# Three small edits to an adaLN transformer block: an earlier second normalisation, one maximum moved inside three steps, five casts moved from VectorE to ScalarE

## The chip, the cores and the metric

The kernel runs on one core of one Trainium2 chip. A core has a matrix engine (TensorE, PE in the profile), VectorE (DVE), ScalarE (ACT), GpSimd (POOL) and SyncE (SP), which here issues most of the DMA transfers. PSUM holds matmul results, SBUF everything else; a PSUM bank holds 512 float32 numbers on each of 128 partitions. The metric is the device time of one execution in microseconds, lower is better.

## The reference, cut to what matters

```python
mod = (silu(c) @ w_mod).reshape(1, 6, 1, -1)
sa, ca, ga, sb, cb, gb = (mod[:, i] for i in range(6))
h = layernorm(x) * (1 + ca) + sa                 # x: 1 x 2048 x 448
q, k, v = split(h @ wqkv)                        # 16 heads of 28 columns
o = softmax(q @ k.T * 28 ** -0.5) @ v
x = x + ga * (o @ wo)
h = layernorm(x) * (1 + cb) + sb                 # first norm of the second half
y = layernorm(h)                                 # second norm
x = x + gb * (gelu(y @ w1 + b1) @ w2 + b2)       # w1: 448 x 1792, w2: 1792 x 448
```

Float32 accuracy is reached by splitting each factor of most products into a high part rounded to the matrix format (`hi`) and the remainder (`lo`), and adding three products: hi·hi, hi·lo and lo·hi.

## The kernel before, in words

**Three stretches.** Up to about 170 us the kernel computes the first norm, the projections to q, k and v and the first part of the row maxima. From there to about 814 us runs the attention loop, and from there to the end the feed-forward part ("the tail").

**The attention loop.** Its outer loop runs over 16 *units*: unit u is (group g of four heads, query block qt of 512 queries), u = 4g + qt. Inside a unit 16 *steps* (kt) run over key blocks of 128 keys; step number = 16u + kt. A step computes the scores of four heads in two halves of two heads each (line 1305), two exponentials of 128 x 2 x 512 on ScalarE (line 1318), and then the four products of the step before with v (function `av`, line 1263). A head has 28 columns, so a score matmul uses only one of four groups of 32 rows of the matrix engine, and matmuls in different row groups can run at the same time. Half 0 lies in row groups 0 and 1, half 1 in row groups 2 and 3. Each half takes three terms (hi·hi, lo·hi, hi·lo), so a step has 12 score matmuls, two at a time in one half.

**Row maxima.** The softmax needs the maximum of each row before its unit begins. For later units these are computed inside the steps as extra matmuls (line 476) into a small ring of PSUM tiles, each followed by a maximum on VectorE (line 481, or line 686 for two heads at once). `emit_single(half, ...)` takes one waiting maximum, preferably one whose row groups are those of the given half. From step 121 on the kernel is in *ring* mode: a third score tile, s2, takes the two PSUM banks of the ring tile m2, and a step has one single maximum and one pair. The flag `three` is set when no maximum is left, near step 236.

**Projection steps.** When a unit of the last group ends, and also unit 11, its result is divided by the softmax sums and multiplied with `wo`. `unit_end_tasks` spreads this over steps of the next unit: `t_den` (kt 1) and `t_rec` (kt 2) send the sums through memory and take reciprocals, `t_split` (kt 6) multiplies on GpSimd (line 1019), `t_split2` (kt 7) makes hi (a cast, line 1029) and lo (a subtraction on GpSimd, line 1030), and four calls of `t_wo` (kt 8 to 11) multiply with `wo`, one token block of 128 each. A unit is `staged` when its result is only stored for later; units 11 to 15 are not staged. In the steps kt 8 to 11 of units 12, 13 and 14 (`is_wo`), ring mode is off: s2 gives its banks back to m2, and a step has `WO_MAX` = 3 single maxima. `n0` of them are emitted beside the scores of the first half, one behind each of its terms and preferring half 1; the other `n_max - n0` stand behind the last scores of the second half and prefer half 0. For unit 15's results the same tasks run inside the tail.

**Second half.** `ln2_stages(b)` gives, for one of four token blocks b of 512 tokens, the work of the two norms as 14 numbered stages: statistics (0 to 3), first norm with scale and shift (`mid`, 4 to 7), statistics again (6 to 9), second norm (`fin`), and the addition of the output bias (`addb`, 10 to 13, GpSimd). `chunk(k)` then transposes four 128 x 128 tiles on TensorE, copies the result as hi on ScalarE (line 1118) and takes lo on VectorE (lines 1120 and 1122). For b = 0 stage i runs at step 231 + i and the chunks at steps 244 to 247. For b = 1, 2, 3 the stages run beside the 14 feed-forward steps of the block before (stage i in step i), and the chunks at step 13. A feed-forward step is `mlp1` (11 matmuls, line 396, a gelu on ScalarE, hi and lo) and `mlp2` of two steps earlier (12 matmuls, lines 1389 to 1391). `w_prep` splits the weights w1 and w2 on VectorE and ScalarE in the last attention unit and during block 0 of the tail.

**Order.** The order on every engine is the order in which the program issues; each engine works through its own instructions in that order and waits on semaphores. `sched` maps a step to small functions that run at the step's end, in the order in which they were registered.

Of the kernel before, what the change touches and what calls it, by code (L numbers as in the profile page):

```python
# [44 lines left out]
def tile_adaln_block(ctx: ExitStack, tc: tile.TileContext, x, wqkv, wo, w1, b1, w2, b2, c, w_mod, out):  # L45
    nc = tc.nc
    pe, act, dve, pool, sp = nc.tensor, nc.scalar, nc.vector, nc.gpsimd, nc.sync
# [27 lines left out]
    def nm(t):  # L75
        uid[0] += 1
        return f"{t}_{uid[0]}"

    def sbt(tag, shape, dt=F32, bufs=1):
        return sb.tile(shape, dt, tag=tag, name=nm(tag), bufs=bufs)  # L80
# [27 lines left out]
    def ps_mx():  # L108
        mx_ring.append(mx_ring.pop(0))
        return ps_tile(mx_ring[-1], 1 if mx_ring[-1] == "m1" else 2)  # L110

    def ps_o():
        return ps_tile("o")
# [4 lines left out]
    def f(t):  # L118
        return t.bitcast(F32)
# [78 lines left out]
    def ln_stat(mv, t, src):  # L198
        st = sbt("st", [128, 6], bufs=2)
        dve.bn_stats(out=st, in_=src)  # L200
        dve.bn_aggr(out=mv[:, t, :], in_=st)

    def ln_rstd(mv, n):
        ve = sbt("ve", [128, 4], bufs=2)
        dve.tensor_scalar(out=ve[:, :n], in0=mv[:, :n, 1], scalar1=EPS, scalar2=None, op0=ALU.add)
        rs = sbt("rs", [128, 4], bufs=2)
        pool.tensor_tensor(out=rs[:, :n], in0=ve[:, :n], in1=neg_half[:, :n], op=ALU.pow)
        return [(mv[:, t, 0:1], rs[:, t : t + 1], rs) for t in range(n)]
# [7 lines left out]
    def normalise(dst, src, mr):  # L216
        dve.tensor_scalar(out=dst[:, :D], in0=src, scalar1=mr[0], scalar2=mr[1], op0=ALU.subtract, op1=ALU.mult)

    def xn_t():
        return sbt("xn", [128, 512], bufs=4)  # L220
# [54 lines left out]
    def transposes(p, xs, k):  # L275
        for t in range(4):
            pe.transpose(p[:, t * 128 : (t + 1) * 128], xs[t][:, k * 128 : (k + 1) * 128], ident)  # L277
# [114 lines left out]
    def mm_acc(p, terms, mid=None):  # L392
        for i, (a, b) in enumerate(terms):
            if mid and i == len(terms) // 2:
                mid()
            pe.matmul(p, a, b, start=(i == 0), stop=(i == len(terms) - 1))  # L396
# [588 lines left out]
    def last_g(qt):  # L985
        return NG - 2 if qt == NB - 1 else NG - 1
# [8 lines left out]
    def unit_end_tasks(u, o_sb):  # L995
        g, qt = divmod(u, NB)
        st = {}
        staged = g < last_g(qt)
        parts = [g] if g > last_g(qt) else list(range(g + 1))

        def t_den():
            q_ = pool if u == NU - 1 else sp
            den = sbt("den", [128, 16], bufs=2)
            q_.dma_start(den, o_sb[DH:128:32, :].rearrange("j (q r) -> j q r", r=16))
            st["den"] = den

        def t_rec():
            q_ = pool if u == NU - 1 else sp
            rec = st["den"]
            dve.reciprocal(rec, rec)  # L1010
            drec = dr.tile([4, 512], F32, tag="drec", name=nm("drec"), bufs=2)
            q_.dma_start(drec.rearrange("j (q r) -> (j q) r", r=16), rec)
            rb = sbt("osb", [128, 512], bufs=2)
            q_.dma_start(rb, drec[:, None, :].broadcast_to([4, 32, 512]))
            st["rb"] = rb

        def t_split():
            st["on"] = st["rb"]
            pool.tensor_tensor(out=st["on"], in0=o_sb, in1=st["rb"], op=ALU.mult)  # L1019

        def t_split2():
            on = st["on"]
            if u < NU - 1:
                hi = sbt("hi", [128, 512], F32R, bufs=3)
                lo = sbt("lo", [128, 512], F32R, bufs=3)
            else:
                hi = sb.tile([128, 512], F32R, tag=YTAGS[7], name="o_hi", bufs=1)
                lo = sbt("osb", [128, 512], F32R, bufs=2)
            dve.tensor_copy(hi, on)
            pool.tensor_tensor(out=lo, in0=on, in1=f(hi), op=ALU.subtract)  # L1030
            st["hi"], st["lo"] = hi, lo
            if staged:
                for part in range(2):
                    sp.dma_start(f(doh[part][g])[:, qt * 512 : (qt + 1) * 512], f((hi, lo)[part]))

        def t_wo(t):
            def go():
                if t == 3 and mx_ring[0] == "m1" and len(mx_ring) > 1:
                    mx_ring.append(mx_ring.pop(0))
                p = ps_mx()  # L1040
                ts = slice(t * 128, (t + 1) * 128)
                terms = []
                for g_ in parts:
                    if g_ == g:
                        hi, lo = st["hi"][:, ts], st["lo"][:, ts]
                    else:
                        hi, lo = o_in[(qt, g_)][:, 0, ts], o_in[(qt, g_)][:, 1, ts]
                    w_hi, w_lo = wo_p[0][:, g_, :], wo_p[1][:, g_, :]
                    terms += [(hi, w_hi), (hi, w_lo), (lo, w_hi)]
                mm_acc(p[:, :D], terms)  # L1050
                y = sbt("full", [128, 512], bufs=3)[:, :D]
                act.copy(y[:, :D], p[:, :D])
                pool.tensor_tensor(out=acc[qt][:, t, :], in0=acc[qt][:, t, :], in1=y[:, :D], op=ALU.add)

            return go


        times = (0, 3, 9, 10) if staged else (0, 1, 5, 6)
        tasks = list(zip(times, (t_den, t_rec, t_split, t_split2)))
        if not staged:  # L1060
            tasks += [(7 + t, t_wo(t)) for t in range(4)]
        return tasks
# [4 lines left out]
    def ln2_stages(b):  # L1067
        h2 = []
        ys = []

        mv = {}
        mr = {}

        def stat(which, t):
            if t == 0:
                mv[which] = sbt("mv", [128, 4, 2], bufs=2)
            ln_stat(mv[which], t, acc[b][:, t, :] if which == 0 else h2[t])
            if t == 3:
                mr[which] = ln_rstd(mv[which], 4)

        def mid(t):
            yt = xn_t()
            ys.append(yt)
            y = yt[:, :D]
            normalise(y, acc[b][:, t, :], mr[0][t])
            pool.tensor_tensor(out=y, in0=y, in1=rows["cb"], op=ALU.mult)
            pool.tensor_tensor(out=y, in0=y, in1=rows["sb"], op=ALU.add)
            h2.append(y)

        def fin(t):  # L1090
            normalise(ys[t], h2[t], mr[1][t])
            dve.tensor_copy(ys[t][:, D:512], ys[t][:, 384:D])

        def addb(t):
            pool.tensor_tensor(out=acc[b][:, t, :], in0=acc[b][:, t, :], in1=rows["b2g"], op=ALU.add)

        plan = {}
        for t in range(4):
            plan.setdefault(t, []).append(lambda t=t: stat(0, t))
            plan.setdefault(4 + t, []).append(lambda t=t: mid(t))  # L1100
            plan.setdefault(6 + t, []).append(lambda t=t: stat(1, t))
            plan.setdefault(11 + t // 2, []).append(lambda t=t: fin(t))
            plan.setdefault(10 + t, []).append(lambda t=t: addb(t))

        def stage(i):
            for fn in plan.get(i, ()):
                fn()

        def chunk(k):
            if b not in yT:  # L1110
                tiles = [
                    sb.tile([128, 512], F32R, tag=YTAGS[(7 * b + n) % len(YTAGS)], name=nm("y"), bufs=1) for n in range(7)
                ]
                yT[b] = (lambda k: tiles[k] if k < 3 else tiles[6], lambda k: tiles[3 + k])
            p = ps_o() if b and k == 3 else ps_mx()
            transposes(p, ys, k)
            hi = yT[b][0](k)
            act.copy(hi, p)
            if k < 3:
                dve.tensor_tensor(out=yT[b][1](k), in0=p, in1=f(hi), op=ALU.subtract)  # L1120
            else:
                dve.tensor_tensor(out=hi[64:128], in0=p[64:128], in1=f(hi)[64:128], op=ALU.subtract)

        return stage, chunk
# [79 lines left out]
    at(28, b2_mul)  # L1204
    last0 = NKT * (NU - 1)
    lnst = [ln2_stages(b) for b in range(NB)]
    for i in range(14):
        at(last0 - 9 + i, lambda i=i: lnst[0][0](i))
# [30 lines left out]
    def is_wo(s_):  # L1239
        return s_ // NKT >= NU - NB and 8 <= s_ % NKT < 12  # L1240
# [30 lines left out]
    for u in range(NU):  # L1271
        g, qt = divmod(u, NB)
        for kt in range(NKT):
            step = u * NKT + kt
# [15 lines left out]
            more = ring and not three and extra(step)  # L1290
            late_one, after = after, more
            n_max = 0 if ring else WO_MAX if is_wo(step) else 4 - step % 2
            n0 = 1 if step % 4 == 3 and not is_wo(step) else 2
            closing = bool(px_open) and step % 2 == 1

            ks, qs = kst[(g, kt // 4)], qst[u]
# [159 lines left out]
```

## Time and profile before

| what | value |
|---|---|
| median of three runs | 1110.67 us (1110.44 to 1110.94) |
| the profiled execution's own time | 1110.93 us |
| its span, first to last instruction | 1109.0 us |
| granted TensorE clock | 1.000 |
| busy share PE / DVE / ACT / POOL | 99% / 72% / 63% / 19% |
| attention loop | about 172 to 814 us |
| tail | about 814 us to the end |

In the profile, a row of the timeline gives the start in us from the span's start, the duration, engine and line, operation, the tile written and the tiles read, shapes, the number of merged instructions, and in brackets the idle time before it and what ended that. A row of the waits gives the total idle time, the number of times and the longest. The busy share of PE is not a measure of full use, because matmuls are pipelined and their ends modelled; distances between starts are what can be read.

### The profile page before, as it was taken

The numbers are of one execution on the slowest core, as the hardware profiler recorded it, in microseconds if no ns is written. First come the engines' busy times: TensorE is split into PE (matmuls) and PEld (weight loads), VectorE is DVE, ScalarE is ACT, GpSimd is POOL, SyncE is SP. The second block draws the span as 40 slices with busy tenths as digits, with TensorE's granted clock in tenths as the row PEclk, the third lists the DMA queues.
The fourth block names the chain that finished last, engine by engine and source line by source line (L and its number), as shares of the span: only waits on it lengthen the run. The fifth ranks groups of instructions, "written<-read, shape, count | busy, mean of one in ns | idle before, by whom it ended". The sixth has DMA issues, their size and how long they took to land.

```text
span 1109.0 us, 20702 instructions
## 1 busy us (share of the span) xinstructions
PE 1098.7 (99%) x8319; PEld 667.0 (60%) x8319; DVE 800.4 (72%) x1380; ACT 701.6 (63%) x892; POOL 213.0 (19%) x214
## 2 busy tenths in 40 slices
PE   8999999999999999999999999999999999999998
PEld 6756775444444444444444454545568888888887
DVE  6968788999999999988888867584557744434322
ACT  4565657888888888888888878577763411111210
POOL 1533333110000000000000020216215414023000
PEclk9999999999999999999999999999999999999999
DMA  9563264121231211221211402112222100000000
GB/s 309 205 199 97 89 202 113 53 68 30 79 92 44 79 34 54 67 89 49 79 40 59 126 29 87 58 30 78 73 82 67 32 34 1 4 31 1 34 1 34
DMA packets 49341, 81.19 MB, mean 73 GB/s; under 512 B 12311, under 2 KB 18702, under 8 KB 49234
## 3 DMA queue, kind: packets, MB, share of 16 engines
q1 hardware_dynamic: 48762, 79.14, 22.7%
q8 instruction: 65, 1.06, 0.4%
q10 hardware_dynamic: 148, 0.46, 0.1%
q0 software_dynamic: 336, 0.28, 0.1%
q14 instruction: 30, 0.25, 0.1%
HBM read 55.04 MB, written 26.48 MB: 74 GB/s over the span
## 4 chain that ended last, share of the span: by engine, by line
PE 96%; DVE 2%; ACT 1%; DMA 1%; issue 1%; SPq 0%; POOL 0%; ACTq 0%; DVEq 0%; POOLq 0%
PE s L1305 23%; PE o L1263 23%; PE m L396 17%; PE pa L396 9%; PE m L476 8%; PE s L1390 3%; PE s L1391 3%; PE s L1389 3%; PE s L476 2%; PE t L1390 1%; PE t L1391 1%; PE t L1389 1%; PE o L277 1%; DMA slot_c<-in_w_mod_dram 1%; DVE mxp L481 1%
## 5 line engine op out<-in xcount | busy, mean ns | idle before, releaser
L481 DVE TENSOR_REDUCE mxp<-m 128x1 f32<-128x512 f32 x563 | 365.0, 686 | 75.3 <-PE m L476 65.2
L1305 PE MATMUL s<-slot_b,slot_a 28*128 28x512 f32 (+1 forms) x3072 | 358.1, 424 | 0.3 <-ACT slot_c0h L1318 0.3
L1305 PEld LDWEIGHTS s<-slot_b,slot_a 28*128 28x128 f32 (+1 forms) x3072 | 211.4, 184 | 172.1 <-ACT slot_c L1318 93.8
L476 PE MATMUL m<-kh,qh 28*128 28x512 f32 x615 | 229.7, 468 | 0.6 <-DVE mxp L481 0.3
L1318 ACT ACTIVATE slot_c<-s 128x1024 f32<-128x1024 f32 x170 | 174.7, 1027 | 53.4 <-PE s L1305 52.5
L1263 PE MATMUL o<-slot_c,v 128*32 128x512 f32 x680 | 178.9, 605 | 0.0
L1351 ACT ACTIVATE full<-m,b_col 128x512 f32<-128x512 f32 x56 | 38.5, 688 | 193.4 <-PE m L396 180.9
L1263 PE MATMUL o<-slot_c0h,v 128*32 128x512 f32 x512 | 134.7, 605 | 0.0
L1263 PE MATMUL o<-slot_c1h,v 128*32 128x512 f32 x512 | 134.7, 605 | 0.0
L1318 ACT ACTIVATE slot_c0h<-s 128x1024 f32<-128x1024 f32 x128 | 131.6, 1028 | 2.4 <-PE m L396 2.4
L1318 ACT ACTIVATE slot_c1h<-s 128x1024 f32<-128x1024 f32 x128 | 130.8, 1022 | 0.0
L686 DVE TENSOR_REDUCE mxp<-s 128x2 f32<-128x1024 f32 x103 | 126.3, 1226 | 5.1 <-PE s L1305 0.2
L1354 DVE CAST hi<-full 128x512 fp32r<-128x512 f32 x42 | 18.6, 444 | 122.8 <-ACT full L1351 122.8
L1318 ACT ACTIVATE slot_d<-s 128x1024 f32<-128x1024 f32 x86 | 88.4, 1027 | 26.3 <-PE s L1305 25.6
L476 PEld LDWEIGHTS m<-kh,qh 28*128 28x128 f32 x615 | 92.2, 182 | 16.8 <-DVE mxp L481 13.3
L1263 PE MATMUL o<-slot_d,v 128*32 128x512 f32 x344 | 90.5, 605 | 0.4 <-ACT osb L1227 0.4
L1019 POOL TENSOR_TENSOR osb<-osb,osb 128x512 f32<-128x512 f32 x16 | 20.5, 1284 | 365.2 <-DMA osb<-drec 334.8
L396 PE MATMUL m<-y,slot_a 128*128 128x512 f32 x160 | 60.7, 396 | 0.0
L1355 DVE TENSOR_TENSOR lo<-full,hi 128x512 fp32r<-128x512 f32 x56 | 42.4, 758 | 20.5 <-ACT hi L1354 16.5
L481 DVE TENSOR_REDUCE mxp<-ma 128x1 f32<-128x512 f32 x61 | 39.5, 682 | 13.2 <-PE ma L476 7.5
L650 DVE CUSTOM_DVE_ANT_0 slot_d0i<-m,slot_d0i 128x512 f32<-128x512 f32 x54 | 37.3, 691 | 15.1 <-PE m L476 9.2
L1263 PEld LDWEIGHTS o<-slot_c,v 128*32 128x32 f32 x680 | 24.6, 108 | 39.1 <-issue 36.5
(343 smaller groups left out, 1854.4 us busy)
## 6 DMA issues: line engine op xcount, KB each, us to landing
slot_b<-d SPq DMA_DIRECT2D x32, 256.0 KB
slot_a<-d SPq DMA_DIRECT2D x32, 256.0 KB
d<-lo SPq DMA_DIRECT2D x28, 256.0 KB
d<-hi SPq DMA_DIRECT2D x16, 256.0 KB
osb<-drec SPq DMA_DIRECT2D x15, 256.0 KB
out_dram<-xn SPq DMA_DIRECT2D x16, 224.0 KB
raw<-in_B_w_dram SPq DMA_DIRECT2D x14, 224.0 KB
qh<-d SPq DMA_DIRECT2D x12, 256.0 KB
```

Of the source, the lines that this page charges most:

```text
L396: pe.matmul(p, a, b, start=(i == 0), stop=(i == len(terms) - 1))
L476: pe.matmul(m, qh_sb[(g, qt)][js, i * 128 : (i + 1) * 128], k[js, :], start=True, stop=True)
L481: dve.tensor_reduce(out=mxp[(g, qt)][:, i, j, cch : cch + 1], in_=m, op=ALU.max, axis=AX.X)
L686: dve.tensor_reduce(out=mxp[(g, qt)][:, i, j : j + 2, cch], in_=t, op=ALU.max, axis=AX.X)
L1263: pe.matmul(o[32 * j : 32 * j + 32, :], v_sb[kt // 4][:, kt % 4, 4 * g + j, :], p[j // 2][:, j % 2, :], start=(kt == 0), stop=(kt == NKT - 1),
L1305: pe.matmul(s2[:, jj, :], ks[rows_, kp, kc], qs[rows_, qp, :], start=(term == 0), stop=(term == 2))
L1318: act.activation(pt[hf], s2, AF.Exp, scale=SCALE)
L1351: act.activation(gf, p, AF.Gelu_apprx_tanh, bias=b1_col[:, i : i + 1])
L1355: dve.tensor_tensor(out=glo, in0=gf, in1=f(ghi), op=ALU.subtract)
L1389: pe.matmul(pp, ghi[:, ts], w_hi, start=(m == 0), stop=False)
L1390: pe.matmul(pp, ghi[:, ts], w_lo, start=False, stop=False)
L1391: pe.matmul(pp, glo[:, ts], w_hi, start=False, stop=(m == NFT - 1))
```

## The change

Three edits, independent of each other in the code:

1. `t_split2`: for units that are not staged (11 to 15) the cast of the 128 x 512 result to `hi` is issued by ScalarE (`act.copy`) and no longer by VectorE.
2. `ln2_stages`: `fin(t)` runs at stage 10 + t // 2 and no longer at 11 + t // 2, for all four blocks.
3. The attention loop: in the first projection step of a unit (kt 8 in an `is_wo` step) `n0` is 1 and no longer 2. It acts where ring mode is off, in steps 200, 216 and 232: one maximum stands beside the first half's scores and two behind the second half's.

```diff
-            dve.tensor_copy(hi, on)
+            (dve.tensor_copy if staged else act.copy)(hi, on)
             pool.tensor_tensor(out=lo, in0=on, in1=f(hi), op=ALU.subtract)
...
-            plan.setdefault(11 + t // 2, []).append(lambda t=t: fin(t))
+            plan.setdefault(10 + t // 2, []).append(lambda t=t: fin(t))
             plan.setdefault(10 + t, []).append(lambda t=t: addb(t))
...
-            n0 = 1 if step % 4 == 3 and not is_wo(step) else 2
+            n0 = 1 if (kt == 8 if is_wo(step) else step % 4 == 3) else 2
```

## The prediction

> **What bounds the kernel now.** I read the page first, for the engine that ends the span, then TensorE's waits, then the timeline around each edited place.
>
> ```profile
> span 1109.0 us, 20702 instructions
> ...
> PE 96%; DVE 2%; ACT 1%; DMA 1%; issue 1%; SPq 0%; POOL 0%; ACTq 0%; DVEq 0%; POOLq 0%
> ```
>
> The chain that ended last runs 96% through TensorE (PE). So an edit counts only where it moves a start on PE; time taken from or given to VectorE (DVE) or ScalarE (ACT) is free until PE waits for it. PE's waits name two places that the edits touch:
>
> ```profile
> PE m L277 <- DVE xn L217: 0.9, 2, 0.6
> ...
> PE m L396 <- POOL lo L1030: 0.3, 1, 0.3
> ```
>
> The first is a transpose waiting for a second norm, the second a projection waiting for lo. They give idle time only; what a wait costs is read from starts. The third place shows in the starts alone. Step 216, a first projection step (kt 8), on PE, ACT and DVE:
>
> ```profile
> 694.70 0.49 PE L1305 MATMUL s<-slot_b,slot_a 29*128 29x512 f32 x2
> ...
> 695.03 0.39 PE L1305 MATMUL s<-slot_b,slot_a 28*128 28x512 f32 x2
> 695.40 0.49 PE L476 MATMUL m<-kh,qh 28*128 28x512 f32 x1
> ...
> 696.52 0.62 PE L1263 MATMUL o<-slot_c1h,v 128*32 128x512 f32 x2
> ...
> 694.33 1.02 ACT L1318 ACTIVATE slot_c1h<-s 128x1024 f32<-128x1024 f32 x1
> 695.97 1.02 ACT L1318 ACTIVATE slot_d<-s 128x1024 f32<-128x1024 f32 x1 [0.62 <-PE s L1305]
> ...
> 693.81 1.23 DVE L686 TENSOR_REDUCE mxp<-s 128x2 f32<-128x1024 f32 x1
> ```
>
> The second maximum starts at 695.40, 0.05 after step 215's second exponential ended (694.33 + 1.02 = 695.35). That exponential reads s2, whose banks the ring tile m2 has just taken over. First score to first product with v: 696.52 - 694.70 = 1.82. The next step has the same 15 matmuls and no such wait:
>
> ```profile
> 700.16 0.49 PE L1305 MATMUL s<-slot_b,slot_a 29*128 29x512 f32 x2
> 700.17 0.51 PE L476 MATMUL m<-kh,qh 28*128 28x512 f32 x2
> 700.50 0.65 PE L1305 MATMUL s<-slot_b,slot_a 28*128 28x512 f32 x8
> ...
> 700.98 0.41 PE L1305 MATMUL s<-slot_b,slot_a 28*128 28x512 f32 x2
> 701.32 0.62 PE L1263 MATMUL o<-slot_d,v 128*32 128x512 f32 x2
> ```
>
> It takes 701.32 - 700.16 = 1.16: four rounds of up to four matmuls, the last three 0.24 apart ((700.98 - 700.50) / 2), 0.34 from the last round to the product. Steps 200 and 232 are as slow as 216:
>
> ```profile
> 650.29 0.50 PE L1305 MATMUL s<-slot_b,slot_a 29*128 29x512 f32 x2
> ...
> 652.12 0.62 PE L1263 MATMUL o<-slot_c1h,v 128*32 128x512 f32 x2
> ...
> 741.46 0.49 PE L1305 MATMUL s<-slot_b,slot_a 29*128 29x512 f32 x2
> ...
> 743.38 0.62 PE L1263 MATMUL o<-slot_c1h,v 128*32 128x512 f32 x2
> ```
>
> They take 1.83 and 1.92.
>
> **The maximum (n0 = 1).** Only steps 200, 216 and 232 change; nothing is added or removed. The second maximum now stands behind all scores, so the wait for the exponential no longer stops the scores. Next in line is the second half's score tile s0: the pair maximum of step 215 reads it until 693.81 + 1.23 = 695.04. With the 0.05 seen above, the second half starts at 695.09, its two further terms at 695.33 and 695.57, and the product at 695.91, 1.21 from the step's start. By then m2 is free (695.35), so the two late maxima go in the last round, in row groups 0 and 1. Savings: 1.82 - 1.21 = 0.61; with the same shape 0.62 and 0.71 in steps 200 and 232; together 1.94. Both ends: if the s0 wait held the rest up as the old one did, only the earlier release is left, 695.35 - 695.04 = 0.31 a step, 0.93 in all; if nothing waits, all three fall to 1.16, 2.09 in all; if the two late maxima shared a row group, 0.24 a step would go again. I take 1.94, since all waits in it have rows. Their reductions on DVE come later, but the ring tile is needed only in the next step, behind the projection.
>
> One thing speaks against this. If matmuls began strictly in program order, the second half could not begin ahead of the first half's third term, the step would take a fifth round, 1.16 + 0.24 = 1.40, and the three steps would save 1.37. Step 217 bears on it: its second maximum, issued behind the second term's pair, starts at 700.17, ahead of that pair at 700.50. I stay with that row. The Trainium skill, "TensorE: Matmul & The Clock Gate", section The mechanism, states the strict order, in starts and in ends; by it the sum would be 0.57 smaller, and the starts of this trace do not agree with it.
>
> **The cast on ScalarE.** Five casts of 0.42 leave DVE, five of about 0.6 come to ACT (a row of such a cast, 0.59, is below). Behind each on ACT stand the next step's exponentials; it waits for GpSimd's product. Where it pays is step 248:
>
> ```profile
> 787.88 0.59 ACT L1118 CAST y<-m 128x512 fp32r<-128x512 f32 x1
> 788.55 1.02 ACT L1318 ACTIVATE slot_c<-s 128x1024 f32<-128x1024 f32 x1
> ...
> 784.47 1.28 POOL L1019 TENSOR_TENSOR osb<-osb,osb 128x512 f32<-128x512 f32 x1 [7.21 <-DMA osb<-drec]
> 790.87 1.34 POOL L1030 TENSOR_TENSOR lo<-osb,hi 128x512 fp32r<-128x512 f32 x1 [5.12 <-DVE hi L1029]
> ...
> 790.30 0.42 DVE L1029 CAST hi<-osb 128x512 fp32r<-128x512 f32 x1
> ...
> 791.40 0.56 PE L396 MATMUL m<-slot_e,hi 128*128 128x448 f32 x2
> 792.26 0.47 PE L396 MATMUL m<-slot_e,lo 128*128 128x448 f32 x1 [0.30 <-POOL lo L1030]
> 792.66 0.76 PE L1305 MATMUL s<-slot_b,slot_a 29*128 29x512 f32 x8
> ...
> 796.51 0.57 PE L396 MATMUL m<-slot_e,hi 128*128 128x448 f32 x2
> ...
> 797.22 0.74 PE L1305 MATMUL s<-slot_b,slot_a 29*128 29x512 f32 x8
> ```
>
> GpSimd's product is ready at 785.75, but DVE reaches the cast only at 790.30, behind the splitting of w1; lo follows at 790.87 to 792.21, and PE waits. From the products with hi to the next scores it takes 1.26 (792.66 - 791.40), against 0.71 in step 249 (797.22 - 796.51): 0.55 lost. ACT is free for the cast at 787.88 + 0.59 = 788.47 and done near 789.07; lo is ready near 790.5, before its matmul's turn 0.4 after 791.40. The price is on ACT: the exponential of 788.55 moves to about 789.1. Its result is read one step later, behind the projection and the scores of 792.66, so nothing waits. I take 0.55 saved; the ends are 0.55 and 0.
>
> In steps 199, 215 and 231 the cast falls into ACT's idle 0.62 ahead of 695.97 (same shape, three times): 695.35 + 0.6 = 695.95, where the exponential starts today, though by the first edit it could start earlier; again its reader stands behind a projection. That idle time and the projection are the cover; were they gone, each cast would cost PE 0.6, 3.0 for five. In the tail (unit 15) the cast stands four feed-forward steps ahead of its projection, on an ACT that waits for PE's next result: 0.
>
> **The norm one stage sooner.** Nothing is added; four normalisations and four small copies a block move up on DVE, past one feed-forward step's work. They issue no DMA. PE rows at the boundary of blocks 0 and 1, then of 1 and 2, then DVE:
>
> ```profile
> 880.75 0.38 PE L277 MATMUL m<-ident,xn 128*128 128x128 f32 x2
> ...
> 882.93 0.45 PE L1389 MATMUL s<-slot_d0i,hi 128*128 128x448 f32 x1
> ...
> 886.25 0.48 PE L396 MATMUL m<-y,slot_b 128*128 128x512 f32 x1
> ...
> 953.98 1.03 PE L277 MATMUL m<-ident,xn 128*128 128x128 f32 x8
> 954.77 0.45 PE L1389 MATMUL s<-slot_d0i,hi 128*128 128x448 f32 x1
> ...
> 880.37 1.33 DVE L217 TENSOR_SCALAR xn<-xn,mv,rs 128x448 f32<-128x448 f32 x1
> ...
> 885.01 1.29 DVE L1120 TENSOR_TENSOR y<-m,y 128x512 fp32r<-128x512 f32 x2
> ```
>
> Eight transposes take 2.18 (882.93 - 880.75) at the first boundary and 0.79 (954.77 - 953.98) at the second: 1.39 lost, because DVE normalises the third tile only at 880.37. One stage sooner all four are done a feed-forward step (some 5 us) before. What is late next: the first matmuls of block 1 (886.25) would come 1.39 sooner, at 884.86, but their PSUM tile is that of the first transposes, which DVE reads from 885.01 for half of 1.29, until about 885.65. The chain up to there hangs on block 0's last gelu, which doesn't move. So they start near 885.7 and 0.55 is saved; the ends are 1.39 and 0. In blocks 2 and 3 PE doesn't wait here: 0. For block 0 the stages fall in steps 241 and 242, where two more normalisations now stand ahead of unit 14's reciprocal on DVE, and behind it on SP its DMAs, then weight loads:
>
> ```profile
> 777.23 0.24 DVE L1010 RECIPROCAL den<-den 128x16 f32<-128x16 f32 x1
> ...
> 778.49 0.20 DVE L1092 COPY xn<-xn 128x64 f32<-128x64 f32 x1
> ...
> 871.09 0.69 DVE L1355 TENSOR_TENSOR lo<-full,hi 128x512 fp32r<-128x512 f32 x1 [4.40 <-ACT hi L1354]
> ```
>
> What follows the reciprocal until 778.69 goes ahead of it: it comes 778.69 - 777.47 = 1.2 later, and so does GpSimd's product, 786.95 for 785.75: still 1.5 before ACT's turn at 788.47. Cost 0. In stage 10 of block 1 the first normalisations wait for GpSimd's reciprocal square root; DVE is idle there for 4.40, ahead of 871.09, which takes them even at 1.33 each. In blocks 2 and 3 the cover is the same, a feed-forward step between two stages; were it gone, lo would come up to 2.7 late, against two steps until mlp2 reads it.
>
> **Sum.** 1.94 + 0.55 + 0.55 = 3.04. The profiled execution took 1110.93, 0.26 above the median and 1.93 above its span; all three savings lie inside the span, so 1107.89 for that execution and 1107.6 against the median 1110.67. A change of 0.2%, 2.2 us, is about what a measurement of this kernel can tell from none.
>
> **Rivals.**
>
> *The second half waits anyway (no change).* s0 blocks as m2 did: 0.93 for 1.94, in all 2.03, 1108.6. For it: a blocked matmul held up everything behind it at 695.40. Against: s0's release comes 0.31 sooner, and only the second half stands behind it. The same side is reached if either of the 0.55 fails and the maxima give less than 1.7: 1108.5 to 1109.7.
>
> *Strict program order on PE (faster, less).* 1.37 + 0.55 + 0.55 = 2.47, 1108.2, with the rows of step 217 against it. It is what the Trainium skill's section named above would make of this kernel.
>
> *The maxima fall out of step (slower).* The two late maxima are taken for the other half, so the order of all later maxima shifts, in steps 200 to 235. Where two matmuls that ran side by side then need the same row group, the step takes a fifth round, 0.24. Above 13 such steps of 36 the gain of 3.04 is gone; at 22 the kernel is over 0.2% slower; in all 36 it is 1110.67 - 3.04 + 8.64 = 1116.3. For it: the order is made by a planner that nothing in the profile shows for the new order. Against: it asks for a half's own maxima first, and the four projection steps now take seven of one half and five of the other, where they took eight and four.
>
> *ACT is held up (slower).* If GpSimd's product in step 247 came more than 1.5 later than I put it, ACT would stand, and past 2.8 PE too, 1 for 1; past six the gain is gone. For it: GpSimd already idles 7.21 for the transfer ahead of 784.47. Against: only 1.2 of delay has a row.
>
> **How the numbers follow.** My sum 0.62, strict order 0.13: faster 0.75. The second half waits, or a 0.55 fails: 0.13, same. Maxima out of step 0.10, ACT held up 0.02: slower 0.12. The time is my sum's, 1107.6. The low end takes the best ends, 2.09 + 0.55 + 1.39 = 4.03: 1106.6. The high end goes into the cases of no change, 1109.6, and leaves out those of slower and a part of the others.
>
> **What would show it.** Steps 200, 216, 232: first score to first product near 1.2, one L476 in the first round, and no matmul waiting for an exponential; near 1.4 is strict order, near 1.5 the s0 wait. Step 248: the wait for lo gone from PE's list, ACT's cast between 788 and 789 less what was saved before. First block boundary: eight transposes in 0.8, the wait for xn gone, and a new one of some 0.8 for L1120 ahead of block 1's first matmul. Steps 201 to 235 otherwise as long as before. I am wrong if those steps grow, if ACT idles ahead of a cast, or if DVE's earlier normalisations, which wait for GpSimd's reciprocal square root, make mlp2 wait for lo.

## The result and the profile after

The changed kernel takes 1108.99 us (median of 18 runs, 1108.13 to 1109.51) against 1110.81 us for the kernel before on the same chip (18 runs, 1109.99 to 1111.58). The ratio is 0.9983 with a 95% interval of 0.9976 to 0.9990: 1.8 us less, a gain, since the interval leaves out 1, but smaller than the 2.2 us that the prediction took for what can just be told from no change. The profiled execution took 1109.11 us, its span is 1107.1 us, and the granted clock is 1.000 as before.

The chain that ended last:

```profile
PE 97%; DVE 1%; DMA 1%; ACT 1%; issue 0%; SPq 0%; ACTq 0%; DVEq 0%
```

TensorE still sets the time. Its list of waits (total, times, longest):

```profile
PE m L396 <- DVE y L1120: 0.5, 1, 0.5
...
PE s L476 <- DVE mxp L481: 0.4, 1, 0.4
```

The waits for xn (L217) and for lo (L1030) are gone from the list, and these two are new. The first was forecast as what is late next at the block boundary; the second was not forecast at all. The three edited places, one after the other. Step 216 on PE, then ACT and DVE:

```profile
694.15 0.50 PE L1305 MATMUL s<-slot_b,slot_a 29*128 29x512 f32 x2
694.16 0.50 PE L476 MATMUL m<-kh,qh 28*128 28x512 f32 x1
694.49 0.79 PE L1305 MATMUL s<-slot_b,slot_a 28*128 28x512 f32 x8
694.99 0.49 PE L476 MATMUL m<-kh,qh 28*128 28x512 f32 x2
695.11 0.40 PE L1305 MATMUL s<-slot_b,slot_a 28*128 28x512 f32 x2
695.44 0.62 PE L1263 MATMUL o<-slot_c1h,v 128*32 128x512 f32 x2
...
693.92 1.02 ACT L1318 ACTIVATE slot_c1h<-s 128x1024 f32<-128x1024 f32 x1
...
693.26 1.23 DVE L686 TENSOR_REDUCE mxp<-s 128x2 f32<-128x1024 f32 x1
```

One maximum stands in the first round, the other two in one of the last, and no score waits for the exponential of 693.92 any more. From the first score to the first product it takes 695.44 - 694.15 = 1.29, where it took 1.82. Steps 200 and 232 do the same:

```profile
650.52 0.49 PE L1305 MATMUL s<-slot_b,slot_a 29*128 29x512 f32 x2
...
651.81 0.62 PE L1263 MATMUL o<-slot_c1h,v 128*32 128x512 f32 x2
...
740.90 0.50 PE L1305 MATMUL s<-slot_b,slot_a 29*128 29x512 f32 x2
...
742.18 0.62 PE L1263 MATMUL o<-slot_c1h,v 128*32 128x512 f32 x2
```

They take 1.29 and 1.28, for 1.83 and 1.92. With starts in thousandths the three savings are 0.54, 0.54 and 0.65, together 1.73.

Step 248, PE, then ACT and POOL:

```profile
790.61 0.57 PE L396 MATMUL m<-slot_e,hi 128*128 128x448 f32 x2
791.02 0.36 PE L396 MATMUL m<-slot_e,lo 128*128 128x448 f32 x1
791.31 0.52 PE L1305 MATMUL s<-slot_b,slot_a 29*128 29x512 f32 x4
...
787.09 0.59 ACT L1118 CAST y<-m 128x512 fp32r<-128x512 f32 x1
787.55 0.64 ACT L1029 CAST hi<-osb 128x512 fp32r<-128x512 f32 x1
788.07 1.05 ACT L1318 ACTIVATE slot_c<-s 128x1024 f32<-128x1024 f32 x1
...
788.27 1.29 POOL L1030 TENSOR_TENSOR lo<-osb,hi 128x512 fp32r<-128x512 f32 x1 [2.23 <-ACT hi L1029]
```

lo is ready at 788.27 + 1.29 = 789.56, well ahead of its matmul at 791.02, and the products with hi are followed by the next scores after 791.31 - 790.61 = 0.70, where it took 1.26: 0.56 saved. The exponential behind the cast comes later and nobody waits for it.

The boundary of blocks 0 and 1, PE, then DVE:

```profile
879.43 1.03 PE L277 MATMUL m<-ident,xn 128*128 128x128 f32 x8
880.22 0.45 PE L1389 MATMUL s<-slot_d0i,hi 128*128 128x448 f32 x1
...
884.33 0.50 PE L396 MATMUL m<-y,slot_b 128*128 128x512 f32 x1 [0.54 <-DVE y L1120]
...
882.92 0.62 DVE L1172 TENSOR_TENSOR slot_e<-full,slot_e 128x448 fp32r<-128x448 f32 x1 [0.63 <-ACT slot_e L1171]
883.58 1.89 DVE L1120 TENSOR_TENSOR y<-m,y 128x512 fp32r<-128x512 f32 x3
```

The eight transposes take 880.22 - 879.43 = 0.79, where they took 2.18. From them to block 1's first matmul it is 884.33 - 879.43 = 4.90, where it was 886.25 - 880.75 = 5.50: 0.60 saved of the 1.39. The other 0.79 is lost again to L1120, 0.54 of it recorded as idle.

These three come to 1.73 + 0.56 + 0.60 = 2.89. What the kernel gained can be read without the noise of its first 640 us, in which nothing is changed: from the first score of step 196 to the end of the last matmul. The first and last of these rows, before and after:

```profile
641.26 0.50 PE L1305 MATMUL s<-slot_b,slot_a 29*128 29x512 f32 x2
...
1104.73 0.36 PE L1391 MATMUL t<-slot_e,lo 128*128 128x448 f32 x1
```

```profile
641.50 0.49 PE L1305 MATMUL s<-slot_b,slot_a 29*128 29x512 f32 x2
...
1102.82 0.36 PE L1391 MATMUL t<-slot_e,lo 128*128 128x448 f32 x1
```

That is 463.83 before and 461.68 after: 2.15 less. (The unchanged part ahead took 0.24 more in this execution, so that the spans differ by 1.9.) This distance, called *the stretch* below, is used for all experiments, because their differences are below what the times can tell. So some 0.7 went again, and the second new wait says where to look. Step 220, PE, then DVE:

```profile
713.41 0.49 PE L476 MATMUL m<-kh,qh 28*128 28x512 f32 x1
713.41 0.49 PE L1305 MATMUL s<-slot_b,slot_a 29*128 29x512 f32 x2
713.42 0.49 PE L476 MATMUL m<-kh,qh 28*128 28x512 f32 x1
...
714.77 0.49 PE L476 MATMUL s<-kh,qh 28*128 28x512 f32 x2 [0.39 <-DVE mxp L481]
...
715.21 0.62 PE L1263 MATMUL o<-slot_d,v 128*32 128x512 f32 x2
...
713.94 0.69 DVE L481 TENSOR_REDUCE mxp<-m 128x1 f32<-128x512 f32 x1 [2.85 <-PE m L476]
```

The same step before:

```profile
714.58 0.49 PE L1305 MATMUL s<-slot_b,slot_a 29*128 29x512 f32 x2
714.58 0.49 PE L476 MATMUL m<-kh,qh 28*128 28x512 f32 x1
...
715.76 0.62 PE L1263 MATMUL o<-slot_d,v 128*32 128x512 f32 x2
```

It took 715.76 - 714.58 = 1.18 and now takes 715.21 - 713.41 = 1.80. There is one more maximum in it (two L476 in the first round, where there was one), and the pair of maxima behind it waits until 713.94 + 0.69 = 714.63, when DVE has read the first of the two. Behind that pair stands the last term of the second half's scores (714.78), and behind it the product.

Read from the program's order, this is what happens. Steps 200 and 216 now take two of their three maxima from half 0, and so the planner works through the waiting maxima in another order. Unit 14's last maximum (group 3, query block 2) was taken in step 216 before. Now it is left over until step 220, which is kt 12 of unit 13, the deadline (`LAST_MAX`), and `finish_max` issues it there ahead of the step's own. It goes into the ring tile m2, in the very step in which ring mode returns and s2 takes m2's banks back, so the pair, which goes into s2, must wait until DVE has read it. Steps 233 and 234 are longer too. Step 233, then step 234:

```profile
745.80 0.50 PE L1305 MATMUL s<-slot_b,slot_a 29*128 29x512 f32 x2
745.81 0.51 PE L476 MATMUL m<-kh,qh 28*128 28x512 f32 x2
746.14 0.88 PE L1305 MATMUL s<-slot_b,slot_a 28*128 28x512 f32 x10
746.86 0.39 PE L476 MATMUL m<-kh,qh 28*128 28x512 f32 x1
747.18 0.62 PE L1263 MATMUL o<-slot_c,v 128*32 128x512 f32 x2
...
750.82 0.49 PE L1305 MATMUL s<-slot_b,slot_a 29*128 29x512 f32 x2
750.83 0.49 PE L476 MATMUL m<-kh,qh 28*128 28x512 f32 x1
...
751.16 0.39 PE L476 MATMUL m<-kh,qh 28*128 28x512 f32 x1
...
752.17 0.62 PE L1263 MATMUL o<-slot_c,v 128*32 128x512 f32 x2
```

Step 233 takes 747.18 - 745.80 = 1.38, where it took 1.14, and step 234 takes 1.35, 0.20 more than before. By then only maxima of half 1 are left. In step 233 the third one, which stands behind the second half's scores, needs a row group of these same scores and makes a fifth round, at 746.86. Step 234 has only two maxima left, since one was taken in step 220, and both stand beside the first half's scores (750.83 and 751.16). By the program's order both are of the same head, so with that head's three score terms its row group has five matmuls, and the step again takes a fifth round. What counts is thus how many matmuls one row group gets, not how many maxima the step has. Against this stand steps 213 to 215, which are 0.19 shorter by the new order. So the account of the stretch, from the starts of every step, is: -1.73 in steps 200, 216 and 232, -0.56 in step 248, -0.60 at the boundary, +0.61, +0.24 and +0.20 in steps 220, 233 and 234, -0.19 in steps 213 to 215; together -2.03 of the -2.15.

### The profile page after: what moved, and what is told of

The parts are those of the page before. It is cut to its first block, busy times and chain, and to the rows that moved or that the text cites. A ratio compares the mean times of both kernels' runs of the same rounds, so it can differ in the third digit from the quotient of the medians.

```text
span 1107.1 us, 20699 instructions
## 1 busy us (share of the span) xinstructions
PE 1097.3 (99%) x8319; PEld 666.5 (60%) x8319; DVE 799.5 (72%) x1375; ACT 703.8 (64%) x897; POOL 212.4 (19%) x214
## 4 chain that ended last, share of the span: by engine, by line
PE 97%; DVE 1%; DMA 1%; ACT 1%; issue 0%; SPq 0%; ACTq 0%; DVEq 0%
PE o L1263 23%; PE s L1305 23%; PE m L396 17%; PE pa L396 9%; PE m L476 8%; PE s L1390 3%; PE s L1391 3%; PE s L1389 3%; PE s L476 2%; PE t L1390 1%; PE t L1391 1%; PE t L1389 1%; DMA slot_c<-in_w_mod_dram 1%; PE o L277 1%; DVE mxp L481 1%; PE ma L476 0%
## 5 line engine op out<-in xcount | busy, mean ns | idle before, releaser
L481 DVE TENSOR_REDUCE mxp<-m 128x1 f32<-128x512 f32 x563 | 364.6, 685 | 75.0 <-PE m L476 56.2
L476 PE MATMUL m<-kh,qh 28*128 28x512 f32 x615 | 228.2, 468 | 0.5 <-DVE mxp L481 0.3
L476 PEld LDWEIGHTS m<-kh,qh 28*128 28x128 f32 x615 | 91.5, 182 | 15.8 <-DVE mxp L481 13.4
L481 DVE TENSOR_REDUCE mxp<-ma 128x1 f32<-128x512 f32 x61 | 39.5, 681 | 13.2 <-PE m L476 8.1
```

Source lines behind the costliest of these rows:

```text
L476: pe.matmul(m, qh_sb[(g, qt)][js, i * 128 : (i + 1) * 128], k[js, :], start=True, stop=True)
L481: dve.tensor_reduce(out=mxp[(g, qt)][:, i, j, cch : cch + 1], in_=m, op=ALU.max, axis=AX.X)
```

## The experiments

The theory to be tested: each edit saves what its own rows show, nothing is lost between them, and the third edit also costs about 0.85 by the order of the maxima, not by its placement. The rivals: the edits take gains from each other (the cast adds to ScalarE what the maximum needs, or the norm holds DVE up), or steps 220, 233 and 234 have a cause of their own.

**The edits alone.** The first kernel has the cast alone.

```diff
-            dve.tensor_copy(hi, on)
+            (dve.tensor_copy if staged else act.copy)(hi, on)
```

> Only the cast on ScalarE. Account theory (each edit gives its own saving, read from TensorE's starts): 0.55 us less, all of it in step 248; the steps 200, 216, 220, 232, 233 and 234 as in the kernel before. Rival (the losses seen in steps 220, 233 and 234 of the changed kernel come from ScalarE's added casts): steps 220, 233 and 234 longer by 0.6, 0.24 and 0.2 here too, and the time not better than before.

1110.27 us (11 runs), a ratio of 0.9997 (0.9988 to 1.0005). The stretch is 463.25, 0.58 less, and step 248 alone is shorter, by 0.56.

The second has the norm alone.

```diff
-            plan.setdefault(11 + t // 2, []).append(lambda t=t: fin(t))
+            plan.setdefault(10 + t // 2, []).append(lambda t=t: fin(t))
```

> Only the second norm one stage sooner. Account theory: 0.6 us less, at the boundary of blocks 0 and 1: eight transposes in 0.8 for 2.2, then a new wait of about 0.55 for L1120. Rival (the saving there needs the other edits' earlier TensorE): no wait goes, the time as before.

1110.61 us (11 runs), 0.9998 (0.9989 to 1.0007). The stretch is 463.27, 0.56 less. Its eight transposes start at 881.05 without a wait between them, and its first matmul of block 1 follows 4.90 later, at 885.95, behind a wait for L1120 of 0.54 as in the changed kernel.

The third has the maximum alone.

```diff
-            n0 = 1 if step % 4 == 3 and not is_wo(step) else 2
+            n0 = 1 if (kt == 8 if is_wo(step) else step % 4 == 3) else 2
```

> Only the maximum moved. Account theory: 0.54, 0.54 and 0.65 saved in steps 200, 216 and 232, 0.2 more in steps 213 to 215, and 0.61, 0.24 and 0.20 lost again in steps 220, 233 and 234, because the order of the maxima shifts: 0.9 us less in all. Rival (those losses belong to the other edits): 1.7 to 1.9 us less, with steps 220, 233 and 234 as before.

1110.04 us (11 runs), 0.9994 (0.9985 to 1.0003). The stretch is 462.96, 0.87 less: steps 200, 216 and 232 are 0.55, 0.56 and 0.65 shorter, and steps 220, 233 and 234 longer by 0.62, 0.25 and 0.20. In step 220 the pair of maxima waits for L481 again, by 0.40.

The three stretches add up to 0.58 + 0.56 + 0.87 = 2.01, against 2.15 for all edits together. They take nothing from each other, and the loss belongs to the third edit. None of the three times by itself could be told from the kernel before.

**The order without the placement.** This kernel is the one before, but its second early maximum in steps 200, 216 and 232 is chosen as the moved one is, preferring half 0. It stands where it stood.

```diff
-                        emit_single(1, ps_mx)
+                        emit_single(0 if term and is_wo(step) and kt == 8 else 1, ps_mx)
```

> Placement as in the kernel before (two maxima beside the first half's scores in steps 200, 216 and 232), but the second one is chosen from half 0, so that the order of the maxima is that of the changed kernel. Account theory: the 0.61, 0.24 and 0.20 in steps 220, 233 and 234 appear without the savings, 0.2 saved in steps 213 to 215, about 0.85 us more in all. Rival (the losses come with the placement or from an earlier TensorE): as before.

1111.30 us (11 runs), 1.0003 (0.9995 to 1.0012). The stretch is 464.21, 0.38 more. Steps 220, 233 and 234 grow by 0.62, 0.24 and 0.20, as in the changed kernel (0.61, 0.24 and 0.20), and steps 213 to 215 shrink by 0.18. In step 220 the pair waits for L481 by 0.38:

```profile
715.45 0.49 PE L476 MATMUL s<-kh,qh 28*128 28x512 f32 x2 [0.38 <-DVE mxp L481]
```

So the loss comes with the choice of the half, wherever the maximum stands. The whole is less than the 0.85 expected, since steps 200, 216 and 232 are also 0.23, 0.09 and 0.16 shorter in this kernel. The starts in step 200 show why. When the waiting maximum is of half 1, it shares a row group with all three terms of the second half's scores, and four rounds start from the end of the wait on (651.00, 651.34, 651.57 and 651.80). When it is of half 0, its row group has only one term left, and there are three (651.07, 651.41 and 651.64, in this kernel). Steps 216 and 232 save the same round, but their waits end somewhat later.

**The loss taken back.** The changed kernel with one more rule in the planner: from step 200 on, maxima of the unit that is due first go first.

```diff
-        m = (alone or same[-2:] or fits or near)[0]
+        mine = [m for m in alone if m[:2] == near[0][:2]]
+        m = ((mine or same[-2:] if clock[0] >= 200 else ()) or alone or same[-2:] or fits or near)[0]
```

> The changed kernel, with the planner told from step 200 on to finish the unit whose maxima are due first. The maximum that was forced out in step 220 is taken in step 214 or before. Account theory: step 220 back from 1.80 to about 1.2 from first score to product, so 0.6 us less than the changed kernel; steps 233 and 234 keep their fifth round (0.24 and 0.20), since by then too few maxima of half 0 are left. Rival (step 220 is long for the switch of the tile s2 itself, not for the forced maximum): step 220 stays at 1.8.

1107.67 us (7 runs), 0.9971 (0.9961 to 0.9982) against the kernel before. The stretch is 461.22, 0.46 less than the changed kernel's; up to step 254 it is 0.56 less, and the tail gives 0.10 back. Step 220 has a single maximum beside the first half again and no wait (lines are one further down in this kernel):

```profile
712.39 0.50 PE L1306 MATMUL s<-slot_b,slot_a 29*128 29x512 f32 x2
712.39 0.49 PE L476 MATMUL m<-kh,qh 28*128 28x512 f32 x1
...
713.52 0.62 PE L1264 MATMUL o<-slot_d,v 128*32 128x512 f32 x2
```

713.52 - 712.39 = 1.13, for 1.80. Steps 233 and 234 stay at 1.36 and 1.37; in this order both have three maxima, all of half 1. The forced maximum was the cause of step 220's loss, and only of that one.

**What holds L1120.** In the changed kernel's boundary rows above, the last thing on DVE ahead of L1120 is L1172, a piece of w2 being split, which waits for ScalarE. This kernel splits that last piece one feed-forward step sooner.

```diff
-            for _ in range(2 if n % 2 else 1):
+            for _ in range(2 if n % 2 or n == 12 else 1):
```

> The changed kernel, with the last piece of w2 split one feed-forward step sooner (step 12 for 13 of block 0), which takes two operations on VectorE and one on ScalarE from ahead of L1120. Account theory (the norm's saving is cut by VectorE's L1120, which stands behind that piece): the wait of 0.54 for L1120 goes, 0.55 us less than the changed kernel. Rival (the wait hangs on the last gelu of block 0 alone): the wait stays above 0.4.

1108.16 us (9 runs), 0.9976 (0.9966 to 0.9985) against the kernel before. The wait falls from 0.54 to 0.17, and the part from step 254 to the end from 294.26 to 293.98, 0.28 less, half of what was expected. The rows of PE, ACT and DVE:

```profile
882.79 0.49 PE L396 MATMUL m<-y,slot_b 128*128 128x512 f32 x1 [0.17 <-DVE y L1120]
...
879.48 0.57 ACT L1171 CAST slot_e<-full 128x448 fp32r<-128x448 f32 x1 [2.41 <-DVE full L1169]
879.95 0.68 ACT L1351 ACTIVATE full<-m,b_col 128x512 f32<-128x512 f32 x1
...
881.32 0.69 DVE L1355 TENSOR_TENSOR lo<-full,hi 128x512 fp32r<-128x512 f32 x1 [0.62 <-ACT hi L1354]
882.04 1.89 DVE L1120 TENSOR_TENSOR y<-m,y 128x512 fp32r<-128x512 f32 x3
```

The splitting was what held L1120, and by these rows it still does, on a longer way. L1120 starts right behind VectorE's lo of the last gelu (881.32 + 0.69 = 882.01), and that lo waits for ScalarE's cast of the gelu to hi. The gelu itself (879.95) stands behind the moved piece's cast (L1171): it starts 1.69 after the first of the transposes (878.26), where in the changed kernel it started 0.26 after it (879.69 and 879.43). That the rest of the gain went this way is read from the rows; no run here moves the piece further.

**Both together.**

> Both of the two additions at once. Account theory: the two savings add up, 1.15 us less than the changed kernel, about 3.3 us less than the kernel before from the same part of the trace. Rival (what is freed in one place is waited for in another): less than 0.8 below the changed kernel.

1107.44 us (6 runs, 1106.68 to 1108.24), 0.9967 (0.9956 to 0.9979) against the kernel before. The stretch is 460.70, 3.13 less than before and 0.98 less than the changed kernel's: 0.60 of it up to step 254, as the planner's rule alone gave 0.56 there, and 0.38 behind it, where the weights alone gave 0.28. The stretch of the two alone was 0.46 and 0.18 less, since each lost 0.1 in the part that it doesn't touch; this 0.1 is about what two executions differ by there. It is the kernel with the shortest stretch and the lowest median of all; its interval overlaps those of the kernels with one of the two, so that by the times alone it isn't told from them.

**Four of the five casts back on VectorE.**

```diff
-            (dve.tensor_copy if staged else act.copy)(hi, on)
+            (act.copy if u == NU - 2 else dve.tensor_copy)(hi, on)
```

> Of the five casts only that of unit 14 (issued in step 247) on ScalarE; the maximum moved; the norm as in the kernel before. Account theory (only step 248 gains by the cast, the other four are free either way): the maximum's 0.87 and the whole 0.56 of the cast. Rival (the other four casts help or hurt, through VectorE or the exponentials): steps 200, 216 and 232 differ by more than 0.1 from 1.29 from first score to product.

The kernel that ran is the changed one with this line alone, so it has the norm one stage sooner as well, other than its expectation says; it is compared with the changed kernel. 1108.82 us (10 runs), 0.9981 (0.9972 to 0.9991) against the kernel before; the stretch is 461.78, 0.10 more than with all five casts on ScalarE. Steps 200, 216 and 232 are within 0.01 of the changed kernel's. So the cast pays in step 248 only, and those ahead of the exponentials of steps 199, 215 and 231 cost nothing. The 0.10 lies in the tail, where unit 15's cast stands, and is no more than what two executions differ by there.

**The third maximum of steps 233 and 234 spread out.** The kernel with both additions, and from step 233 on two maxima a projection step for three.

```diff
-            n_max = 0 if ring else WO_MAX if is_wo(step) else 4 - step % 2
+            n_max = 0 if ring else WO_MAX - (step > NKT * (NU - 2) + 8) if is_wo(step) else 4 - step % 2
```

> The kernel with both additions, and from step 233 on two maxima a step, beside the first half's scores, for three: the last six are all of half 1. Account theory (a third maximum that needs a row group of the second half's scores costs a fifth round): steps 233 and 234 back from 1.38 and 1.35 to 1.15, step 235 from 0.91 to 1.15, 0.2 us less than with both additions, about 3.5 us less than the kernel before. Rival (the fifth round comes from the ring tiles, not from the row groups): steps 233 and 234 stay near 1.35 and step 235 adds 0.24.

1107.68 us (10 runs), 0.9971 (0.9962 to 0.9980). Step 233 is back to four rounds:

```profile
744.40 0.50 PE L1306 MATMUL s<-slot_b,slot_a 29*128 29x512 f32 x2
...
745.54 0.62 PE L1264 MATMUL o<-slot_c,v 128*32 128x512 f32 x2
```

745.54 - 744.40 = 1.14; step 234 takes 1.14 as well, and step 235 goes from 0.92 to 1.14. So in this planner's order the fifth round was the third maximum of half 1, the second in one row group. The part up to step 254 is 0.24 less than in the kernel with both additions, but the rest is 0.39 more, and the stretch 460.84 for 460.70. At the block boundary the transposes for block 1 end 0.45 earlier on the clock of the trace (its last four start at 881.55 for 882.00), but L1121, which they feed, starts only 0.17 earlier (881.86 for 882.03), and the wait for it is 0.46 again for 0.17. What stands ahead of it is an exchange of weight pieces between DVE and ScalarE, in which each waits for the other and neither for TensorE. That takes back 0.28 of the 0.39; the other 0.1 stays open.

## Why the prediction was right and wrong

The forecast was 1107.6 with a range of 1106.6 to 1109.6. The time lies in the range and 1.4 above the forecast, in what the prediction called "same", which had 0.13. Of the sum's 3.04, 2.15 came in the stretch. That the range still holds the time is in part luck: its high end was drawn for waits that stay, and the loss that came was none of those.

*The cast*: 0.55 forecast, 0.56 measured, 0.58 alone. The mechanism held in each link: ScalarE takes the cast as soon as its copies (L1118) are done, lo comes ahead of its matmul's turn, and the exponential that is put off has no reader in a hurry. The four other casts at nothing held too.

*The norm*: 0.55 forecast, 0.60 measured, 0.56 alone. That the 1.39 would be cut by a wait for L1120 was right, in place and in kind. It costs the 0.79 that is left of the 1.39, as "some 0.8" said, though the list of waits shows 0.54 of it. What holds L1120 was named only in part: "block 0's last gelu" stands ahead of it, but so did the splitting of w2.

*The maximum*: 1.94 forecast, 1.73 measured. The mechanism is the one described: scores of the first half pass, the second half waits for s0, and the two late maxima share a round. The size was off in one figure. The second half starts 0.39 after the step's first score, as computed, when the pair maximum of step 215 ends (693.26 + 1.23 = 694.49). But I put both of the next rounds 0.24 apart, the distance of later rounds. Behind a start that was waited for, the next round comes after 0.34: here 694.54 to 694.88, and the quoted rows of step 217 already showed it at the step's start (700.16 and 700.50). That makes a step of 1.29 for 1.21. The rival of strict order on TensorE gave 1.40 a step; the rows have 1.29, and the second half's first pair starts at 694.54, ahead of the first half's last pair, issued before it, at 694.71. The Trainium skill, "TensorE: Matmul & The Clock Gate", section The mechanism, states that order, and neither kernel's starts bear it out where matmuls lie in different row groups. The rival in which the second half holds up the rest gave 1.5; it isn't seen.

*The order of the maxima*: this is the step that failed. The sum had nothing for it, though the maximum's paragraph says that "Only steps 200, 216 and 232 change". As a rival it had 0.10 and was priced at 0.24 a fifth round, to decide only from 13 steps on. Two such rounds came, 0.44. The other 0.61 is of a kind that the rival did not have: a maximum that misses its turn isn't only taken beside other scores, it is forced at a deadline, and the deadline lies in the step in which the ring tile's banks change hands. The reason given against it, that four projection steps would take "seven of one half and five of the other, where they took eight and four", counted one unit, and took an even split for a good one; what mattered is which unit's maximum is left when its deadline comes, and which row groups the last maxima in the queue need. Together the shift cost 1.05 and gave 0.19 back.

## What to carry to other kernels

Before an edit takes work from another end of a queue, list the queue in the new order up to its last entry, deadlines included: here that was a question to the program, not to the chip, and it would have shown the forced maximum of step 220. Where gains are a thousandth of the time, measure them as the distance between two starts on the engine that sets the end, with an unchanged stretch left out: the runs' times could not tell any of the three edits alone from nothing, while the starts gave each to some hundredths. When a wait goes, take the next one behind it as the new price and look for who holds it: at the boundary it was worth another 0.28 to move a piece of unrelated work by one step, and the rows of that kernel show the same piece still in the way, on another engine.

## What the runs showed of the hardware

- The distance from a step's first round of score matmuls to the second is 0.34 (694.15 to 694.49, 745.80 to 746.14), that between later rounds was 0.24 in step 217. A round that follows a wait inside the step also has 0.34 behind it (694.54 to 694.88). A forecast built on one spacing was off by 0.1 in each of three steps.
- In these steps the length goes by the row group with the most matmuls: with four it was 1.14 (step 233 before), with five 1.38 (step 233 after) and 1.35 (step 234 after, which has one matmul fewer than before).
- A cast of 128 x 512 to the matrix format takes 0.64 on ScalarE (787.55) where VectorE took 0.42 (790.30 before). It is slower there, and the kernel faster, because ScalarE comes to it 790.30 - 787.55 = 2.75 sooner by the two traces, of which 0.79 is what the changed kernel is ahead by at that step.
- A wait can cost more than the idle time in brackets: step 220 shows 0.39 and is 0.61 longer, and the boundary before showed 0.9 for xn and lost 1.39.
